# Attention and gated-MLP kernel: the q*k products of four groups summed to one chunk on VectorE, queues planned anew, and the last output group added in order of completion

## The chip, the cores and the metric

One core of a Trainium2 chip. The metric is the device time of one execution in microseconds, as the median of several executions. Two kernels are compared by a ratio: the mean time of one kernel's fast runs over the mean of the other's fast runs of the same rounds, so it is not quite the ratio of the medians that are quoted. A difference under 2% counts as "the same" for a verdict; here the differences are near 1%, and what carries the argument is the ratio's interval and the traces.

Engines: TensorE (PE, matmuls; PEld is its weight load), VectorE (DVE), ScalarE (ACT), GpSimd (POOL), SyncE (SP), which issues nearly all DMAs here.

## The reference, cut to what matters

```python
x = A_x                                   # 2048 tokens, width 512
xn = _layernorm(x)
return x + _A_ref(xn, A_wqkv, A_wo) + _B_ref(xn, B_w_in, B_w_sp, B_b_sp, B_w_out)

# A: attention, 32 heads of 16; each token looks at 8 keys, 0, 2, ... 14 tokens back
logits = jnp.einsum('bhsd,bhswd->bhsw', q, kg) * scale
o = jnp.einsum('bhsw,bhswd->bhsd', softmax(logits), vg)      # then @ wo

# B: gated MLP
z = _gelu(x @ w_in); z1, z2 = z[..., :688], _layernorm(z[..., 688:])
g = jnp.einsum('ts,bsf->btf', w_sp, z2) + b_sp[None, :, None]
return jnp.einsum('bsf,fd->bsd', z1 * g, w_out)
```

## The kernel before

Every engine has its own queue of instructions, and the kernel gives the order of all of them in one long list of tokens; an instruction starts when its queue has come to it and its inputs and buffers are ready. So the list is a plan of every queue at once:

```python
ORDER = """
z1.2 z2.1 p1.3 z0.3 zg1.2 p0.2 zg2.1 q2.3 zg0.3 p1.1 zs2.1 z1.0 p1.2 qc2.3 q2.1 p1.0 zg1.0 p0.0 z2.2 qc2.1
# ... 14 lines cut ...
s1.1 O2 T12 Gi15 A55 A56 A57 Or2 A58 Oh2.0 U15 A59 T15 Oh2.1 F2.0 F2.1 s2.0 O3 F2.2 F2.3 xr3 s2.2 Or3 s2.3
Oh3.0 s2.1 Oh3.1 F3.0 F3.1 s3.0 s3.1
"""
```

`z`/`X` are PE's products for z2 and z1, `q` those for q and k, `V` for v, `G` those of the spatial mix g. On DVE, `p` multiplies q by k, `a` is the pair add below, `N` normalises z2, `A` are the multiplies and adds of softmax weights with v (15 for each of four output groups), `U` is z1*g, `F` adds the residual to the output. `L` are the logits matmuls, `O`, `Or`, `Oh` the three parts of an output group, `T` a DMA transpose of u = z1*g, `xr` and `s` loads of x and stores of the output.

A logit is a sum over 16 dimensions. The products stand as four chunks of 128 partitions (four dimensions of 32 heads each), for 8 groups. DVE adds chunks 2 and 3 to 0 and 1; a selection matmul with `rsel` sums four partitions into one and adds the two chunks in PSUM, the memory that holds PE's results. Four blocks of tokens (`tb`) go into four column strips of 32 of the PE array:

```python
def pair_add(g):
    if g not in PAIRED:                      # PAIRED = all eight
        return
    V.tensor_tensor(pr[g % 3][:, 0:2], pr[g % 3][:, 0:2], pr[g % 3][:, 2:4], ALU.add)

def logits(g):
    o, h = g // 2, g % 2
    pl = ps_aux.tile([P, 4, P], F32, name="pl", tag="aux")
    n_c = 2 if g in PAIRED else C
    for c in range(n_c):
        for tb in range(TB):
            PE.matmul(pl[32 * tb:32 * tb + 32, :, :], rsel[:], pr[g % 3][:, c, :, tb, :],
                      start=(c == 0), stop=(c == n_c - 1), tile_position=(0, 32 * tb))
    tiles["l", g] = pl
```

An output group takes PSUM tiles from the same three-buffer pool as z and g, two blocks of tokens in one tile. In the last group's second half the adds and stores of blocks 2 and 3 follow their matmuls, so they come into DVE's queue before `F3.0 F3.1`, the adds of blocks 0 and 1:

```python
ps_mm = ctx.enter_context(tc.tile_pool(name="ps_mm", bufs=3, space=PSUM))
# ... in out_heads ...
        if tb % 2 == 0:
            pmm = ps_mm.tile([P, 2, TBS], F32, name="po", tag="mm")
        pos.append(pmm[:, tb % 2, :])
# ...
def out_half(o, h):
    if o == 3 and h == 1:
        for tb, part, E in ((2, 0, SP), (3, 0, A), (3, 1, SP)):
            out_full(o, tb, part)            # matmuls
            out_add(o, tb, part)             # DVE
            out_store(o, tb, part, E)        # DMA
    else:
        for tb in (2 * h, 2 * h + 1):
            out_full(o, tb)
```

## Time and profile before

| | before |
|---|---|
| median of 4 runs | 206.69 us (206.44 to 207.16) |
| span of the profiled run | 206.2 us |
| busy: PE, DVE, ACT | 199.2, 180.8, 97.3 us |
| DVE's waits, 25 to 192 us | 8.9 us |
| PE, first z product to last matmul | 177.90 us |
| last matmul to last DVE add, then to the end | 1.63, 2.90 us |

The lines themselves are in the prediction. Two rows need a word. "First z product to last matmul" is taken from PE's timeline (start of the first `pz` row, end of the last `pb` row). I use it below for all kernels, because the start varies between executions whatever the kernel: the first z product begins between 22.4 and 25.0 us in the profiles of this study, as the first loads come sooner or later, and in the two latest (`d1` and `e6`) the granted clock was low as well: 0.55 and 0.60 in the two stretches of 2 us from 8 us on in `d1`, 0.69 and 0.50 in `e6`, against 1.00 in the changed kernel's second profile. The span carries that accident; this length does not. The profiled execution of the kernel before had a late start too and took 207.95 us, 1.26 above the median. In five profiles of this study in which PE's work is the same, it is 176.82 or 176.83 us.

### The profile page before, as it was taken

How to read it: one execution, taken by the hardware profiler on the slowest of the kernel's cores; microseconds unless marked ns; L12 is line 12 of the kernel's file. 1: busy time of each engine (PE TensorE's matmuls, PEld its weight loads, DVE VectorE, ACT ScalarE, POOL GpSimd, SP SyncE). 2: the span in 40 equal slices, each digit the busy share in tenths (PEclk: the TensorE clock that was granted, in tenths of full speed). 3: DMA queues.
4: the chain of work that ended last, by engine and by line, in shares of the span. 5: the costliest groups of instructions: out<-in, count | busy, mean ns of one | idle time of the engine just before them, and what ended most of it. 6: DMA issues, size and time to landing. Idle time of an engine off the chain costs nothing.

```text
span 206.2 us, 4083 instructions
## 1 busy us (share of the span) xinstructions
PE 199.2 (97%) x1695; PEld 126.2 (61%) x1699; DVE 180.8 (88%) x259; ACT 97.3 (47%) x159; POOL 5.6 (3%) x15
## 2 busy tenths in 40 slices
PE   7899999999999999999999999999999999999991
PEld 2598866555566666666566666664566654664650
DVE  3979799899679999969999999999999998589604
ACT  3375998879899787634303755430032230020000
POOL 5000000500000000000000000000000000000000
PEclk9999999999999999999999999999999999999998
DMA  5972547400000693199960599998389000465523
GB/s 137 356 257 53 102 101 239 107 0 0 3 0 3 155 182 73 38 234 224 157 168 21 114 199 181 253 206 188 89 152 235 10 3 0 115 147 167 155 97 103
DMA packets 65826, 25.91 MB, mean 126 GB/s; under 512 B 56208, under 2 KB 65488, under 8 KB 65552
## 3 DMA queue, kind: packets, MB, share of 16 engines
q1 hardware_dynamic: 65360, 25.12, 54.9%
q0 software_dynamic: 80, 0.26, 0.5%
q10 hardware_dynamic: 368, 0.27, 0.5%
q8 instruction: 13, 0.21, 0.5%
q14 instruction: 5, 0.04, 0.1%
HBM read 10.13 MB, written 2.10 MB: 59 GB/s over the span
## 4 chain that ended last, share of the span: by engine, by line
PE 94%; DMA 2%; DVE 1%; issue 1%; DVEq 0%; ACTq 0%
PE pg L448 36%; PE pz L235 18%; PE pq L306 14%; PE po L520 7%; PE pv L409 7%; PE po L496 6%; PE pl L359 2%; DMA r_x<-in_A_x_dram 2%; PE pt L221 1%; PE pa L520 1%; PE po L505 1%; PE pb L496 1%; DVE r_qk L510 1%; PE pa L306 0%; DVEq L687 0%
## 5 line engine op out<-in xcount | busy, mean ns | idle before, releaser
L448 PE MATMUL pg<-z,r_qk 128*128 128x344 bf16 x448 | 67.0, 309 | 0.0
L448 PEld LDWEIGHTS <-r_qk 128*128 128x128 bf16 x448 | 43.8, 98 | 21.8
L235 PE MATMUL pz<-w_z,xnT 128*128 128x344 bf16 x256 | 40.3, 309 | 0.0
L423 DVE TENSOR_TENSOR r_pr<-r_x,r_w 128x2048 bf16<-128x2048 bf16 x32 | 38.2, 1218 | 0.4
L454 ACT ACTIVATE gs<-pg,b_col 128x688 bf16<-128x688 f32 x16 | 13.2, 831 | 53.7 <-PE pg L448 53.6
L427 DVE TENSOR_TENSOR r_pr<-r_pr 128x2048 bf16<-128x2048 bf16 x28 | 33.9, 1216 | 0.1
L235 PEld LDWEIGHTS <-xnT 128*128 128x128 bf16 x256 | 24.8, 98 | 13.8 <-issue 1.2
L340 DVE TENSOR_TENSOR r_pr<-r_qk 128x2048 bf16<-128x2048 bf16 x24 | 28.2, 1218 | 2.5 <-ACT r_qk L316 2.5
L306 PE MATMUL pq<-xnT,r_w 128*128 128x256 bf16 (+1 forms) x176 | 29.7, 323 | 0.0
L306 PEld LDWEIGHTS <-r_w 128*128 128x128 bf16 x184 | 20.5, 115 | 7.5 <-issue 0.6
L316 ACT CAST r_qk<-pq 128x1024 bf16<-128x1024 f32 (+1 forms) x16 | 15.4, 993 | 3.7 <-PE pq L306 3.4
L297 ACT ACTIVATE r_uz<-pz 128x688 bf16<-128x688 f32 x16 | 11.6, 744 | 9.7 <-PE pz L235 9.5
L520 PE MATMUL po<-r_w,r_uz 128*128 128x512 bf16 x66 | 14.9, 379 | 0.6 <-issue 0.6
L409 PE MATMUL pv<-xnT,r_w 128*32 128x512 bf16 x256 | 14.6, 380 | 0.0
L496 PE MATMUL po<-r_lg,r_pr 32*128 32x512 bf16 x224 | 14.5, 375 | 0.0
L520 PEld LDWEIGHTS <-r_uz 128*128 128x128 bf16 x85 | 8.0, 98 | 9.8 <-issue 1.5
L351 DVE TENSOR_TENSOR r_pr<-r_pr 128x4096 bf16<-128x4096 bf16 x6 | 13.5, 2285 | 0.0
L203 DVE BATCH_NORM_STATS2 stats<-r_x 128x6 f32<-128x512 bf16 x16 | 10.8, 673 | 2.1 <-DMA r_x<-in_A_x_dram 2.1
L259 ACT ACTIVATE junk<-z 128x688 bf16<-128x688 bf16 x16 | 12.5, 781 | 0.1
L409 PEld LDWEIGHTS <-r_w 128*32 128x32 bf16 x256 | 9.5, 138 | 4.5 <-issue 0.3
L253 ACT ACTIVATE z<-pz 128x688 bf16<-128x688 f32 x16 | 11.8, 741 | 0.5 <-PE pz L235 0.5
L496 PEld LDWEIGHTS <-r_pr 32*128 32x128 bf16 x272 | 7.6, 93 | 6.5 <-issue 0.9
(80 smaller groups left out, 164.0 us busy)
## 6 DMA issues: line engine op xcount, KB each, us to landing
r_lg<-in_A_wo_dram SPq DMA_DIRECT2D x8, 256.0 KB, 4.1
r_qk<-in_A_x_dram SPq DMA_DIRECT2D x16, 128.0 KB, 2.4
out_dram<-r_qk SPq DMA_DIRECT2D x15, 128.0 KB, 2.1
r_w<-in_A_wqkv_dram SPq DMA_DIRECT2D x3, 512.0 KB, 5.6
r_x<-in_A_x_dram SPq DMA_DIRECT2D x3, 512.0 KB, 6.2
w_z<-in_B_w_in_dram SPq DMA_DIRECT2D x2, 688.0 KB, 6.7
r_w<-in_B_w_out_dram SPq DMA_DIRECT2D x1, 640.0 KB, 5.1
r_x<-in_A_x_dram POOLq DMA_DIRECT2D x1, 256.0 KB, 4.3
```

The source lines that it names most:

```text
L235: PE.matmul(pz[:, hh, 0:FHALF], xnT[:, kc, i * P:(i + 1) * P], wz[:, kc, hh * FHALF:(hh + 1) * FHALF], start=(kc == 0), stop=(kc == C - 1))
L306: PE.matmul(pq[:, cc, p0 * P:(p0 + b1 - b0) * P], wqk[:, sd, kc, c0 + cc:D:C], xv[:, kc, b0:b1, j, :], start=(kc == 0), stop=(kc == C - 1))
L316: cast = A.copy(dst, pq[:, :, p0 * P:(p0 + b1 - b0) * P].rearrange("p c (b t) -> p c b t", b=b1 - b0))
L340: prod = V.tensor_tensor(pr[g % 3][:, c].rearrange("p w b t -> p b w t"), q3.unsqueeze(2).broadcast_to([P, TB, 4, P]), k4, ALU.mult)
L351: V.tensor_tensor(pr[g % 3][:, 0:2], pr[g % 3][:, 0:2], pr[g % 3][:, 2:4], ALU.add)
L409: PE.matmul(pv[32 * tb:32 * tb + 32, dd, :], wv[:, kc, 2 * d2 + dd, :], xnT[:, kc, tb * TBS:(tb + 1) * TBS], start=(kc == 0), stop=(kc == ...
L423: V.tensor_tensor(pw_t[n], vp[:, :, off:off + P], a_sb[:, slot_w(w), ts].unsqueeze(1).broadcast_to([P, DH, P]), ALU.mult)
L427: V.tensor_tensor(pw_t[n] if dst is None else dst, pw_t[n], pw_t[m], ALU.add)
L448: PE.matmul(pg[:, hh, 0:FHALF], wsp[n][:, k, :], z2[:, k, hh * FHALF:(hh + 1) * FHALF], start=(k == 0), stop=(k == NT - 1))
L454: A.activation(gs[:], tiles.pop(("g", n))[:, :, 0:FHALF], ACT.Identity, bias=b_col[:, i:i + 1])
L496: PE.matmul(pc, op[32 * tb:32 * tb + 32, d, o * P:(o + 1) * P], wo_r[32 * tb:32 * tb + 32, d, cs], start=(d == 8), stop=False, tile_positi ...
L520: PE.matmul(pc, uT[:, o % 2, m, tb * P:(tb + 1) * P], wout[:, m, cs], start=False, stop=(m == MCH - 3))
```

## The change

The intent: take matmuls off PE, which is busy from end to end, by one more add on DVE for four of the eight groups; plan all queues anew so that DVE has room for it; and let the last adds go in the order in which their sums are complete.

```diff
-PAIRED = (0, 1, 2, 3, 4, 5, 6, 7)
+CHUNKS = (1, 1, 2, 2, 1, 1, 2, 2)
 ORDER = """
-z1.2 z2.1 p1.3 z0.3 zg1.2 p0.2 zg2.1 q2.3 zg0.3 p1.1 ...        (all 18 lines replaced; cut)
-Oh3.0 s2.1 Oh3.1 F3.0 F3.1 s3.0 s3.1
+z1.3 z0.0 p1.1 z1.1 zg1.3 p0.0 zg0.0 q2.0 zg1.1 p0.1 ...
+A55 s1.3 T9 A56 U12 O2 Gi15 U15 U13 T15 A57 T13 A58 Or2 Oh2.0 T12 A59 Oh2.1 F2.0 F2.1 s2.1 T14 O3 F2.2 F2.3
+xr3 s2.0 Or3 s2.3 Oh3.0 s2.2 Oh3.1 F3.0 F3.1 s3.1 s3.0 end
 """
     def pair_add(g):
-        if g not in PAIRED:
-            return
         V.tensor_tensor(pr[g % 3][:, 0:2], pr[g % 3][:, 0:2], pr[g % 3][:, 2:4], ALU.add)
+
+    def pair_add2(g):
+        V.tensor_tensor(pr[g % 3][:, 0], pr[g % 3][:, 0], pr[g % 3][:, 1], ALU.add)
...
-        n_c = 2 if g in PAIRED else C
+        n_c = CHUNKS[g]
...
     def out_half(o, h):
-        if o == 3 and h == 1:
-            for tb, part, E in ((2, 0, SP), (3, 0, A), (3, 1, SP)):
+        for tb in (2 * h, 2 * h + 1):
+            for part in range(len(tiles["o", o][tb])):
                 out_full(o, tb, part)
-                out_add(o, tb, part)
-                out_store(o, tb, part, E)
-        else:
-            for tb in (2 * h, 2 * h + 1):
-                out_full(o, tb)
+
+    def last_adds():
+        for tb, part, E in ((2, 0, SP), (3, 0, A), (3, 1, SP)):
+            out_add(3, tb, part)
+            out_store(3, tb, part, E)
```

The new tokens `b0 b1 b4 b5` are `pair_add2`, `end` is `last_adds`.

More of the change, by code (lines that the diff above doesn't have):

```diff
@@ L40 @@
 ORD = [1, 2, 3, 0]
-PAIRED = (0, 1, 2, 3, 4, 5, 6, 7)
+CHUNKS = (1, 1, 2, 2, 1, 1, 2, 2)
 ORDER = """
-z1.2 z2.1 p1.3 z0.3 zg1.2 p0.2 zg2.1 q2.3 zg0.3 p1.1 zs2.1 z1.0 p1.2 qc2.3 q2.1 p1.0 zg1.0 p0.0 z2.2 qc2.1
-p0.3 zs1.2 z2.0 p0.1 zg2.2 z0.0 zg2.0 a1 w0 q2.0 zs2.0 zg0.0 a0 z1.1 qc2.0 q2.2 zg1.1 halo zs1.0 p2.3 z3.2
-qc2.2 X1 p2.0 z0.1 Xg1 zg3.2 L1 zs2.2 L0 z2.3 zs3.2 p3.3 zg0.1 z0.2 p3.2 zg2.3 z1.3 p2.2 zg0.2 zs1.1 q3.1 p3.0
-Lc0 Lc1 p2.1 zg1.3 q3.3 zs0.1 p3.1 qc3.1 q3.0 a2 qc3.3 z3.3 qc3.0 a3 q3.2 zg3.3 zs1.3 nw.0 p4.3 z3.0 qc3.2
@@ L47 @@
-zs0.0 X0 p4.0 zs2.3 p4.2 L2 zg3.0 L3 V7 zs0.3 nw.1 p5.3 zs0.2 Xg0 V1 nw.2 p5.0 Lc3 Vc7 nw.3 nw.4 V6 nw.5 nw.6
-p4.1 Vc1 zs3.0 p5.1 z3.1 Vc6 p5.2 X5 Lc2 zg3.1 M0.0 w4 V4 nw.7 zs3.3 nw.8 a4 Xg5 w3 V5 Vc4 st.0 nw.9 nw.10
-M0.1 nw.11 nw.12 w1 V2 st.1 a5 Vc5 zs3.1 L4 w2 Vc2 V0 nw.13 N2.3 N1.0 st.2 N2.2 M0.2 N1.1 L5 N2.1 V3 N0.1 st.3
-Vc0 N0.2 N1.2 N0.3 st.4 N1.3 X4 Vc3 N3.3 N0.0 N3.0 X2 N2.0 N3.1 p7.1 G0.0 p7.3 G0.1 Xg2 N3.2 Xg4 G0.2 p6.2 Lc5
-X3 M0.3 G0.3 p6.0 Xg3 Lc4 G4 p6.3 w6 Gi0 p6.1 late E0 S0.0 G1 p7.0 w10 S0.1 S0.2 p7.2 S0.3 S0.4 Gi4 a6 w8 G3
@@ L52 @@
-Gi1 w5 a7 w9 R0 L6 L7 Lc6 A0 G2 Lc7 Gi3 A1 A2 U3 mask U4 M1.0 G6 wo1.0 A3 wo1.3 wo1.2 M1.1 U0 M1.2 A4 A5 G5 A6
-Gi6 Gi2 M1.3 A7 U1 A8 T1 X8 Gi5 U2 T0 A9 E1 X6 A10 G8 wo0.1 A11 w7 A12 Xg8 wo0.0 Xg6 S1.0 T3 S1.1 X7 A13 G9
-Xg7 A14 w14 Gi8 A15 wo0.3 A16 T2 S1.2 A17 G7 U6 wo0.2 S1.3 U5 wo1.1 S1.4 Gi9 xr0 R1 A18 T4 A19 X9 Gi7 A20 G14
-A21 w11 Xg9 U7 A22 w13 A23 A24 T5 X11 Gi14 A25 O0 Xg11 T7 A26 A27 w15 U8 A28 Or0 Oh0.0 U9 A29 Oh0.1 F0.0 A30
-A31 G10 T8 F0.1 F0.2 F0.3 s0.2 T6 A32 A33 xr1 X10 Gi10 A34 w12 X12 Xg10 A35 G13 Xg12 A36 T9 A37 s0.0 A38 s0.3
@@ L57 @@
-s0.1 A39 X15 A40 Gi13 X14 A41 G11 A42 Xg14 Xg15 A43 A44 A45 U14 X13 Gi11 A46 O1 Xg13 A47 U11 A48 U10 Or1 A49
-Oh1.0 A50 Oh1.1 F1.0 F1.1 G12 F1.2 U13 s1.2 A51 T10 F1.3 T11 T14 G15 Gi12 T13 U12 A52 s1.3 xr2 A53 A54 s1.0
-s1.1 O2 T12 Gi15 A55 A56 A57 Or2 A58 Oh2.0 U15 A59 T15 Oh2.1 F2.0 F2.1 s2.0 O3 F2.2 F2.3 xr3 s2.2 Or3 s2.3
-Oh3.0 s2.1 Oh3.1 F3.0 F3.1 s3.0 s3.1
+z1.3 z0.0 p1.1 z1.1 zg1.3 p0.0 zg0.0 q2.0 zg1.1 p0.1 q2.2 qc2.0 p1.0 p1.3 q2.3 qc2.2 p0.3 z3.1 p0.2 qc2.3
+zs1.1 z0.3 p1.2 zg3.1 z1.2 a0 w0 zg0.3 zs1.3 z1.0 zs0.3 a1 q3.1 zg1.2 w3 zg1.0 halo q2.1 zs0.0 b0 qc3.1 p2.0
@@ new lines @@
+z2.2 qc2.1 b1 z2.0 p2.2 V0 zg2.0 p2.3 zg2.2 zs2.0 L1 L0 z0.1 Vc0 p3.3 Lc0 q3.3 p3.0 zs1.2 zg0.1 p2.1 q3.0
+qc3.3 p3.1 z0.2 a2 qc3.0 zs2.2 z2.3 zg0.2 q3.2 p3.2 zs1.0 zg2.3 a3 z3.0 qc3.2 z3.2 zg3.0 p4.3 zs2.3 z2.1 zg3.2
+p4.1 z3.3 zs0.2 p4.0 zg2.1 X3 zg3.3 nw.0 p4.2 X5 Xg3 nw.1 a4 Lc1 X4 Xg5 zs0.1 L2 zs2.1 V4 p5.3 zs3.1 st.0 Xg4
+nw.2 V3 nw.3 p5.2 Vc4 nw.4 p5.0 zs3.2 L3 V2 zs3.0 nw.5 nw.6 nw.7 Vc3 nw.8 nw.9 nw.10 p5.1 Lc2 V5 Lc3 nw.11 b4
+w4 Vc2 V1 nw.12 Vc5 a5 w2 zs3.3 V7 Vc1 nw.13 st.1 b5 w1 V6 Vc7 N0.0 N1.2 st.2 N1.0 N0.2 L4 L5 N0.3 X7 N1.1
@@ new lines @@
+st.3 N2.0 st.4 Vc6 N0.1 X6 N1.3 N3.1 late N2.3 N3.2 G0.0 N3.0 Xg7 M0.0 G0.1 Xg6 N2.1 M0.1 N2.2 X1 M0.2 N3.3
+p7.1 G0.2 Xg1 M0.3 Lc4 G0.3 p7.3 G1 p6.0 E0 p7.2 Gi0 p6.3 Lc5 p6.2 G4 Gi1 w7 S0.0 p7.0 w6 p6.1 S0.1 xr0 S0.2
+G3 a7 S0.3 S0.4 Gi4 w5 a6 w10 R0 X0 Gi3 U4 L7 T4 L6 G2 A0 Xg0 Lc6 w8 U1 Lc7 U3 U0 A1 A2 X2 Gi2 mask M1.0 G5
+Xg2 A3 A4 A5 A6 X12 M1.1 Gi5 w11 A7 G6 Xg12 A8 wo1.0 w9 A9 M1.2 A10 wo1.1 A11 G7 Gi6 U5 M1.3 T5 U6 A12 E1 A13
+G8 U2 Gi7 A14 T2 A15 T6 S1.0 A16 X10 Gi8 w14 S1.1 X14 A17 T1 A18 G9 Xg10 S1.2 wo1.3 A19 T3 A20 S1.3 A21 T0 G14
@@ new lines @@
+A22 Gi9 wo0.3 wo0.2 A23 Xg14 A24 U7 A25 S1.4 T7 X8 Gi14 A26 wo1.2 X9 wo0.0 wo0.1 A27 w12 G10 A28 Xg9 R1 Xg8
+A29 w13 A30 X13 A31 G11 Xg13 A32 Gi10 A33 U8 A34 A35 X11 Gi11 A36 O0 Xg11 A37 A38 U14 A39 Or0 Oh0.0 A40 A41
+Oh0.1 F0.0 U10 s0.0 F0.1 G13 F0.2 T8 A42 s0.1 F0.3 A43 s0.3 xr1 U11 A44 O1 w15 U9 A45 Gi13 A46 A47 Or1 Oh1.0
+A48 Oh1.1 F1.0 F1.1 A49 s1.1 s0.2 G12 T11 A50 A51 F1.2 F1.3 s1.2 s1.0 A52 xr2 X15 A53 G15 Xg15 A54 T10 Gi12
+A55 s1.3 T9 A56 U12 O2 Gi15 U15 U13 T15 A57 T13 A58 Or2 Oh2.0 T12 A59 Oh2.1 F2.0 F2.1 s2.1 T14 O3 F2.2 F2.3
@@ L650 @@
     st = z2_var(3, 3) + [z2_log, z2_exp]
-    steps = {"z": z2_mm, "zg": z2_gelu, "zs": z2_sq, "q": qk_mm, "qc": qk_cast, "p": prod_c, "a": pair_add,
+    steps = {"z": z2_mm, "zg": z2_gelu, "zs": z2_sq, "q": qk_mm, "qc": qk_cast, "p": prod_c, "a": pair_add, "b": pair_add2,
              "L": logits, "Lc": logits_cast, "V": v_mm, "Vc": v_cast, "X": z1_mm, "Xg": z1_gelu,
@@ L656 @@
              "G": g_mm, "Gi": g_bias, "U": u_mul, "T": u_tr, "A": lambda k: ap[k](),
-             "O": out_heads, "Or": out_rest, "Oh": out_half, "F": out_add, "s": out_store,
+             "O": out_heads, "Or": out_rest, "Oh": out_half, "F": out_add, "s": out_store, "end": last_adds,
              "halo": halo_zero, "wo": load_wo, "late": load_late, "xr": load_xr, "w": load_wsp}
```

## The prediction

> **What bounds the kernel now.** I read the page's busy shares and slices first, then the chain that ended last, then the groups of instructions, then the waits of VectorE (DVE) and its order of time.
>
> ```profile
> PE 199.2 (97%) x1695; PEld 126.2 (61%) x1699; DVE 180.8 (88%) x259; ACT 97.3 (47%) x159; POOL 5.6 (3%) x15
> PE   7899999999999999999999999999999999999991
> DVE  3979799899679999969999999999999998589604
> PE 94%; DMA 2%; DVE 1%; issue 1%; DVEq 0%; ACTq 0%
> ```
>
> Busy shares, slices of 5.2 us, and shares of the chain. TensorE (PE) is busy in every slice but the first and last, and the chain runs through it for 94% of the 206.2 us span. A busy PE need not be at its best, but here no wait for another engine stands between 8 us and 201.7 us: its only idle pieces are four of 0.16 us marked "issue", ahead of the last matmuls of the output groups. So a PE instruction that goes shortens the end, unless a wait opens. DVE at 88% is the runner-up.
>
> The logits stage, from the chain in order of time:
>
> ```profile
> 72.60 0.43 PE pl L359 x8
> 74.75 0.43 PE pl L359 x8
> 99.19 0.98 PE pl L359 x16
> ```
>
> Start, length, what: eight selection matmuls (one group, two chunks) hold PE for 0.43 us, or 54 ns each, though each is recorded at 381 ns. Four run side by side in column strips. The same matmuls between full-width ones take 0.98 us for 16, that is 0.11 us over 16 x 54 ns, and the full-width stretch after such a block is also 0.11 us too long (3.61 us for 24 of L235, which elsewhere take 3.50 us).
>
> The end, from the timeline of all engines and DVE's own (start, length, engine, line):
>
> ```profile
> 200.62 1.07 DVE L510 TENSOR_TENSOR r_qk<-pa,r_qk 128x512 bf16<-128x512 f32 x2 [6.10 <-PE pa L520]
> 201.03 0.64 PE L520 MATMUL pb<-r_w,r_uz 128*128 128x224 bf16 x5
> 201.71 0.39 DVE L510 TENSOR_TENSOR r_qk<-pb,r_qk 128x224 bf16<-128x224 f32 x1
> 202.02 1.28 DVE L510 TENSOR_TENSOR r_qk<-po,r_qk 128x512 bf16<-128x512 f32 x2
> ```
>
> PE ends at 201.67 us. The two `po` adds belong to blocks 0 and 1 of the last group, whose sums are complete some 4 and 3 us before the span's last matmul, since PE does blocks 0, 1, 2, 3 in that order. They are queued behind the adds of 2 and 3, and DVE idles 6.10 us first. That is an order of the queue, not of the data.
>
> The waits of DVE from 25 to 192 us (total, times, longest):
>
> ```profile
> DVE r_uz L462 <- ACT gs L454: 2.7, 1, 2.7
> DVE r_pr L340 <- ACT r_qk L316: 2.5, 1, 2.5
> DVE smt L388 <- ACT r_w L383: 1.8, 1, 1.8
> DVE r_qk L510 <- PE po L520: 0.8, 1, 0.8
> DVE r_uz L340 <- ACT r_qk L316: 0.6, 1, 0.6
> DVE zvar L265 <- ACT junk L259: 0.5, 1, 0.5
> ```
>
> They add to 8.9 us. This is all the room DVE has.
>
> **What the Trainium skill says.** "VectorE: DVE Perf Modes", section "The perf-mode tier table", lists 1224 ns for a bf16 `tensor_tensor` of 2048 elements, with 2x as its ceiling. The trace agrees: 1218 ns for L340 and 1216 for L427. "TensorE: Matmul & The Clock Gate", Part 3, says that small matmuls at different tile positions run concurrently in the array; agreed, 381 ns recorded against 54 ns of PE's time each. So a group's matmul is far cheaper than its record. "Perfetto Trace Analysis", "Identifying the Most-Contended Engine", warns that matmul busy share is a poor measure of distance from the roofline; I therefore rest on the gapless chain, not on the 97%. "DMA: Bandwidth & Descriptors", "Anatomy of one DMA", puts about 2.0 us of fixed cost on a DMA (measured there for GpSimd's path). Output stores here take 2.0 us to landing in the median and 1.5 at least, so the last store's landing can't be removed by this change.
>
> **The change, part by part.**
>
> Logits on PE. Four of eight groups (0, 1, 4, 5) go from two chunks to one: 4 x 4 = 16 matmuls fewer, 16 x 54 ns = 0.87 us. In the new order the column-strip work (logits and v products) falls into three unbroken stretches instead of four; a stretch costs 0.11 us on each side, so another 0.22 us. All of this lies on the path: **1.1 us off PE**.
>
> Adds on DVE. Four `tensor_tensor` of 128x2048 are new. The row says 1218 ns, but starts in a run lie nearer: eight of L340 take 9.17 us, so 1.146 us each. Four cost 4.6 us. They are off the path as long as DVE keeps its appointments. For that I summed the durations along both queues, with no waits, from 23.9 us (PE) and 25.9 us (DVE), in the old and the new order. In the old order DVE's last group-3 sum, which the last heads matmuls need, comes to 182.1 us by this sum; the trace has it end at about 191.4, so 8.9 us of waits and 0.4 of small overhead. PE needs it at 193.1: spare 1.7 us. In the new order the sum gives 186.6, with the overhead 187.0; PE, 1.1 us earlier, needs it at 192.0. So DVE may wait **5.0 us in all** where it now waits 8.9. I think it will wait 2 to 4: the first two new adds are queued ahead of the products of output group 2, and the 2.5 us hole at 54.9 (products waiting for the q/k casts) is just where 2 x 1.146 us fit. Five products instead of three now stand between the softmax maximum and the sum that waits 1.8 us for ScalarE's exponential. The 2.7 us hole before an L462 multiply comes from a g product that is placed earlier, relative to it, in the new order.
>
> Other appointments by the same sums, allowing 1.5 to 2.5 us of waits and overhead so far: the first g products (PE at 78.0 to 82.7) need normalised z2 some 0.5 to 1 us earlier, and have it; the last logits (PE at 99.1) need the last pair add, at 98.5 to 99.2. This one is close. Output groups 0, 1 and 2 start at 151.4, 164.4 and 183.4 and their sums are done by about 124, 146 and 168: wide.
>
> Queues planned anew. The same 16 z2 tiles, 16 z1 tiles, 8 q/k, 8 v, 16 g products and all loads remain; only positions move. It is worth nothing itself: it makes room for the adds. One risk: the last transposes (four of u) now include one queued behind an output store on SyncE, issued near 191 to 192.5; with the 2.7 us that transposes take to land it arrives at 194 to 195.2, against a need at 195.4.
>
> Last group's adds. The matmuls keep their order, the adds of blocks 0 and 1 go ahead. DVE's last add then ends 0.43 us after PE's last matmul (202.10 against 201.67) instead of 1.63 us (203.30): **1.2 us less**. What follows is a store and its landing: 206.2 - 203.3 = 2.9 us now. The last store becomes 56 KB rather than 128 KB, so perhaps 0.3 us less; I count half.
>
> Sum: 1.1 + 1.2 + 0.15 = 2.45 us, on the span 206.2 to 203.75. I take off 0.2 us for small stalls at the close appointments: 206.78 - 2.25, rounded to **204.5 us**, 1.1% less.
>
> **The rivals.** First, DVE becomes the bound: the 4.6 us are not hidden. For it speaks that DVE is busy in nearly every slice from 100 to 175 us and that the close joins have under 1 us to spare. Against it: 8.9 us of holes, and z1 and g work of PE that the new order puts ahead of output group 0 (it starts at 151 instead of 138.8 us), which is what a planner does to gain slack. If all holes stay, 8.9 - 5.0 = 3.9 us of stall arise: 208.4 us. If half stay, none. Second, the saved chunk is hidden or taken back: PE gains 1.1 us and then waits as long for a late transpose or cast, and only the tail remains: 205.5 us. For it speaks that transposes and adds are close; against it that the old order shows the same close margins and not one wait. Third, matmuls are worth what their records say: 16 x 381 ns = 6.1 us, making 199 us. The 0.43 us pieces of the chain rule it out.
>
> **Range and chances.** Main case, PE gapless and the tail shortened by 1.2 to 1.5 us: 204.0 to 204.6. Stalls of up to 1.5 us at the joins: up to 206. Runs of one kernel differ by 0.3 us. So 203.5 to 206.2. Over 2% faster needs under 202.7 us, 1.8 us more than I can find: 0.04. Over 2% slower needs 210.9, more than the first rival in full: 0.02. Within 2%: 0.94.
>
> **What would show it right or wrong.** In the changed profile: 48 matmuls of L359's line instead of 64 and PE's last matmul near 200.6; 12 adds of the pair kind, four with 2048 elements, and DVE's total about 185; the three holes of 2.7, 2.5 and 1.8 us gone or halved; no line of PE waiting for DVE or a DMA between 24 and 199 us; DVE's last instruction a `pb` add, some 0.4 us after PE's end; the span ending 2.6 to 2.9 us after it. I am wrong if PE waits for DVE at the last pair adds (near 99 us) or at the last output group's start (near 192), for a transpose near 195, or if the store's end grows because several stores leave together.

## The result

The changed kernel takes **204.69 us** (median of 4 runs, 204.55 to 205.33) against 206.69. The ratio is 0.9907, 95% interval 0.9879 to 0.9935: within 2%, and clear of 1. Measured again with more rounds on another chip it was 205.02 us and 0.9906 (0.9881 to 0.9932). Its profile, page first; line numbers have moved by one or two (L359 is L360 now, L510 is L511):

```profile
PE 196.2 (97%) x1679; PEld 125.0 (62%) x1683; DVE 185.0 (91%) x263; ACT 102.5 (51%) x163; POOL 18.0 (9%) x15
PE   7799999999999999999999999999999999999993
DVE  4999799999999999999899999999999999988504
```

PE has 16 instructions fewer and the slices stay full. DVE has four more and is at 91%; the softer digits that it had before slice 25 are nearly gone. ACT's 5 us more are four more loads of function tables (ten where there were six, 1.28 us each) that the new order brings, and POOL's 12 us more are one cast of the bias that is recorded at 15.1 us, not 2.8; PE waits for neither after 24 us.

The logits in the chain of work (start, length, what):

```profile
43.67 0.43 PE pl L360 x8
61.05 0.55 PE pl L360 x8
65.05 0.43 PE pl L360 x8
74.12 0.43 PE pl L360 x8
97.99 0.98 PE pl L360 x16
```

48 matmuls in 2.82 us. Before, the chain's five pieces were 64 matmuls in 3.80 us (0.98 twice, 0.43 twice, 0.98).

DVE's waits from 25 to 192 us (total, times, longest):

```profile
DVE r_qk L511 <- PE po L521: 1.6, 2, 0.9
DVE r_uz L463 <- ACT gs L455: 1.3, 1, 1.3
DVE r_pr L424 <- PE pl L360: 0.8, 1, 0.8
DVE zmean L263 <- ACT z L253: 0.4, 1, 0.4
```

4.1 us in place of 8.9. The waits of 2.5 us for the q/k casts and of 1.8 us for the exponential have gone. PE's own waits for other engines after 24 us: none.

The end, from the timeline of all engines:

```profile
197.28 1.29 DVE L511 TENSOR_TENSOR r_qk<-po,r_qk 128x512 bf16<-128x512 f32 x2 [5.12 <-DMA out_dram<-r_qk]
198.48 1.04 DVE L511 TENSOR_TENSOR r_qk<-pa,r_qk 128x512 bf16<-128x512 f32 x2
198.67 0.64 PE L521 MATMUL pb<-r_w,r_uz 128*128 128x224 bf16 x5
199.45 0.38 DVE L511 TENSOR_TENSOR r_qk<-pb,r_qk 128x224 bf16<-128x224 f32 x1
```

The two `po` adds are first now, and the last add ends 0.52 us after PE's last matmul.

Where the time went, in the traces: the span fell by 3.4 us, but 1.28 us of that is the start (first z product at 23.77 us before, 22.49 after), which is chance. The rest is PE's length, 177.90 to 176.82 us (1.08 less), and the way from its last matmul to the last add, 1.63 to 0.52 us (1.11 less); the end after that got 0.07 us longer. 1.08 + 1.11 - 0.07 = 2.12 us, against 2.00 in the medians.

### The profile page after: what moved, and what is told of

Read it like the earlier page. It is cut to its first block, busy times and chain, and to the rows that moved or that the text cites. A ratio compares the mean times of both kernels' runs of the same rounds, so it can differ in the third digit from the quotient of the medians.

```text
span 202.8 us, 4061 instructions
## 1 busy us (share of the span) xinstructions
PE 196.2 (97%) x1679; PEld 125.0 (62%) x1683; DVE 185.0 (91%) x263; ACT 102.5 (51%) x163; POOL 18.0 (9%) x15
## 4 chain that ended last, share of the span: by engine, by line
PE 85%; DMA 4%; SPq 3%; DVE 3%; issue 2%; ACT 1%; ACTq 0%; DVEq 0%
PE pg L449 35%; PE pz L235 19%; PE pq L306 13%; PE pv L410 7%; PE po L521 4%; PE po L497 4%; DMA r_x<-in_A_x_dram 1%; PE pl L360 1%; DMA r_uz<-r_uz 1%; DMA out_dram<-r_qk 1%; SPq L469 1%; DVE r_qk L511 1%; SPq L516 1%; SPq L474 1%; PE pt L221 1%
## 5 line engine op out<-in xcount | busy, mean ns | idle before, releaser
L306 PE MATMUL pq<-xnT,r_w 128*128 128x256 bf16 (+1 forms) x176 | 28.5, 316 | 0.3 <-ACT xnT L225 0.3
L634 POOL CAST b_col<-b 128x16 f32<-128x16 bf16 x1 | 15.1, 15142 | 32.7 <-DMA b<-in_B_b_sp_dram 32.7
L511 DVE TENSOR_TENSOR r_qk<-po,r_qk 128x512 bf16<-128x512 f32 x14 | 9.1, 684 | 6.8 <-DMA out_dram<-r_qk 5.1
```

Source lines behind the costliest of these rows:

```text
L306: PE.matmul(pq[:, cc, p0 * P:(p0 + b1 - b0) * P], wqk[:, sd, kc, c0 + cc:D:C], xv[:, kc, b0:b1, j, :], start=(kc == 0), stop=(kc == C - 1))
L634: G.tensor_copy(b_col[:], b16[:])
```

## The experiments

All kernels gave the right result. The table has for each the median, the ratio to the kernel before in the same rounds with its interval, and from the one profile PE's length as explained above and the way from PE's last matmul to DVE's last add. The lengths with 3 and 6 idle adds are from executions in which the granted clock fell as well; see there.

| kernel | median us | ratio (95%) | PE length us | to last add us |
|---|---|---|---|---|
| before | 206.69 | | 177.90 | 1.63 |
| changed | 204.69 | 0.9907 (0.9879-0.9935) | 176.82 | 0.52 |
| changed, again | 205.02 | 0.9906 (0.9881-0.9932) | 176.82 | 0.43 |
| changed, old ending | 205.97 | 0.9964 (0.9950-0.9978) | 176.82 | 1.63 |
| before, new ending | 205.32 | 0.9937 (0.9924-0.9951) | 177.91 | 0.43 |
| changed, two chunks everywhere | 205.84 | 0.9960 (0.9948-0.9973) | 178.01 | 0.43 |
| before, one chunk in old queues | 207.83 | 1.0055 (1.0042-1.0068) | 179.06 | 1.63 |
| changed + 1 idle add | 204.84 | 0.9903 (0.9872-0.9933) | 176.82 | 0.43 |
| changed + 3 idle adds | 207.33 | 1.0042 (1.0015-1.0068) | 180.77 | 0.43 |
| changed + 6 idle adds | 213.15 | 1.0299 (1.0266-1.0331) | 184.45 | 0.53 |
| changed + 2 idle adds later | 205.35 | 0.9929 (0.9895-0.9963) | 177.28 | 0.43 |
| changed, one transpose early | 204.73 | 0.9895 (0.9871-0.9919) | 176.83 | 0.42 |
| the same, five groups of one chunk | 204.35 | 0.9873 (0.9823-0.9923) | 176.60 | 0.43 |
| the same, six groups | 204.49 | 0.9873 (0.9832-0.9914) | 176.68 | 0.44 |

### The ending, undone and alone

`e1_old_tail`: in the changed kernel, the old `out_half` is put back and `last_adds` does nothing.

```diff
     def last_adds():
-        for tb, part, E in ((2, 0, SP), (3, 0, A), (3, 1, SP)):
-            out_add(3, tb, part)
-            out_store(3, tb, part, E)
+        pass
```

> The changed kernel with the old ending alone: the last output group's adds of blocks 2 and 3 stand ahead of those of 0 and 1 again; all else is new. Theory (the tail is worth what the distance from PE's last matmul to DVE's last add says): that distance goes back from 0.5 to 1.6 us, so 1.1 us slower than the changed kernel (204.7 -> 205.8), ratio to the kernel before 0.995. Rival (the gain is in the matmuls and queues, the tail is hidden behind stores that land late anyway): under 0.4 us slower.

`e2_new_tail_only`: the kernel before, with the new `out_half`, `last_adds` and the token `end`; nothing else.

```diff
-Oh3.0 s2.1 Oh3.1 F3.0 F3.1 s3.0 s3.1
+Oh3.0 s2.1 Oh3.1 F3.0 F3.1 s3.0 s3.1 end
```

> The kernel before with the new ending alone; its queues and its two chunks for all groups stay. Theory: 1.1 us faster than before (206.7 -> 205.6), ratio 0.9945, with DVE's last add 0.5 us after PE's last matmul. Rival (the new ending only pays with the new queues, as the stores of the old order stand in its way): 0 to 0.4 us.

Undone, it costs 1.0 to 1.3 us by the medians (205.97 against 205.02 and 204.69, on other chips) and 1.2 us by the ratios (0.0057 of 206.7). Alone it gives 1.4 us by the medians, 1.3 by the ratio. The way from PE's last matmul to the last add is 1.63 us in every kernel with the old order and 0.42 to 0.53 in every one with the new; PE's length does not move. Both rivals (hidden behind stores; worth something only with the new queues) fall.

### The chunks, undone in the new queues

`e3_two_chunks_new_queues`:

```diff
-CHUNKS = (1, 1, 2, 2, 1, 1, 2, 2)
+CHUNKS = (2, 2, 2, 2, 2, 2, 2, 2)
     def pair_add2(g):
+        if CHUNKS[g] == 2:
+            return
```

> The changed kernel with two chunks for all groups (the four new adds gone, 16 logits matmuls back); new queues and new ending stay. Theory (54 ns a matmul, gapless PE): PE from the first z product to its last matmul grows by 0.87 us, time 205.6, ratio 0.9945; DVE does 4.6 us less and only idles more. Rival A (DVE had become the bound): the time stays or falls though PE has more to do. Rival B (a matmul is worth its record of 381 ns): 6 us slower.

205.84 us, and PE's length grows by 1.19 us, more than the 0.87 expected. The sixteen matmuls account for 0.87 at most, so PE waited. Its weight loads show where (timeline of PEld; in brackets the idle time before and what ended it):

```profile
195.08 0.09 PEld L499 LDWEIGHTS <-r_pr 32*128 32x128 bf16 x1
195.61 0.33 PEld L508 LDWEIGHTS <-r_uz 24*128 24x128 bf16 x8 [0.43 <-DMA r_uz<-r_uz]
```

The transpose of u's tile 14, queued on SyncE behind the first store of group 2 (`s2.1 T14`), came late. Up to the start of the last output group, PE's time is as worked out: 168.98 us from the chain's first z product against 169.20 in `e2`, the 0.22 us that the three column-strip stretches save against four. From there to the last row of matmuls (`pb`) it takes 8.23 us instead of 7.91: 0.32 us of waiting. In the changed kernel the same stretch takes 7.90 us, with no wait. So the transpose that the prediction named as a risk sits on the edge. Rival A (DVE had become the bound) and rival B (381 ns a matmul) fall: DVE does four adds fewer here, and the kernel is slower, by 1.1 us.

Compared with `e2`, which has the same ending and the same matmuls, this run also prices the plan by itself: 178.01 against 177.91 us of PE, so the new queues alone are worth nothing. By the medians this run is even 0.5 us slower than `e2` (205.84 against 205.32), of which 0.1 is PE; in `e2`'s profile the end after the last add is 0.4 us shorter (2.6 against 3.0 us), and why is not shown.

### One chunk without the new queues

`e4_one_chunk_old_queues`: the kernel before with `CHUNKS` and `pair_add2`, and each new add right behind its pair add.

```diff
-p0.3 zs1.2 z2.0 p0.1 zg2.2 z0.0 zg2.0 a1 w0 q2.0 zs2.0 zg0.0 a0 z1.1 ...
+p0.3 zs1.2 z2.0 p0.1 zg2.2 z0.0 zg2.0 a1 b1 w0 q2.0 zs2.0 zg0.0 a0 b0 z1.1 ...
-p4.1 ... nw.8 a4 Xg5 ...      M0.1 ... st.1 a5 Vc5 ...
+p4.1 ... nw.8 a4 b4 Xg5 ...   M0.1 ... st.1 a5 b5 Vc5 ...
```

> The kernel before with one chunk for the same four groups, each new add right after the pair add of its group, old queues and old ending. It asks what the new plan was worth. Theory (8.9 us of DVE's waits soak up most of 4.6 us, but the appointments near 79, 83 and 99 us have under 1 us to spare): PE gets 1 to 2 us of waits for DVE that take the 0.87 us back: 206.5 to 208. Rival (the plan is not needed, the holes take all): 205.9, ratio 0.996, PE without a wait.

207.83 us: slower than the kernel before. PE's waits in this run:

```profile
PE pl L360 <- DVE r_uz L352: 1.2, 1, 1.2
PE po L521 <- issue: 0.6, 4, 0.2
PE pg L449 <- DVE z L289: 0.4, 1, 0.4
```

The logits of a group wait 1.2 us for its second add (L352), and the first g products wait 0.4 us for normalised z2; together with weight loads that start late, PE's length is 179.06 us. That is 1.16 us more than before although 0.87 us of matmuls are gone, so about 2.0 us of waiting was bought. The holes of DVE did take a part: its wait for the casts fell from 2.5 to 0.3 us and the one for the exponential from 1.8 to 0.9. The point is that a hole helps only the appointments behind it. With the adds in these places the old queues can't afford them, and the new plan can; other places in the old queues were not tried.

### How much room has DVE? Adds that nobody reads

To measure the room directly, adds of 128x2048 into a dead weight buffer were put into DVE's queue of the changed kernel, between the weighted v sums A34 and A35.

```diff
-... A33 U8 A34 A35 X11 ...
+... A33 U8 A34 y y y A35 X11 ...
+    scr = w_z2[:].rearrange("p k f -> p (k f)")[:, 0:4 * TBS].rearrange("p (w t) -> p w t", w=4)
+    def idle_add():                                              # token y
+        V.tensor_tensor(scr, a_sb[:, 0:4, :], a_sb[:, 4:8, :], ALU.add)
```

`c0_changed_again` is the changed kernel beside them.

> The changed kernel itself, unaltered, as the yardstick for the runs beside it (its first measurement had few rounds and an interval of 0.6%). All theories: 204.7 us, ratio to the kernel before 0.990 to 0.991.

> The changed kernel with three more adds of 128x2048 on DVE that nobody reads (into a dead weight buffer), in the middle of the weighted v sums; 3.4 us of DVE work. The last sum that PE needs ended 2.8 us ahead of its reader in the changed kernel, and 1.3 us of DVE's waits lie between. Theory (DVE is busy but not the bound): no change, within 0.2 us of 204.7. Rival (at 91% DVE has become the bound): 3.4 us slower, 208.1.

> The same with six idle adds, 6.9 us of DVE work. Theory (room of 2.8 us at the last sum plus 1 to 2 us of waits that close): 2.0 to 3.1 us slower, 206.7 to 207.8, with PE waiting for DVE's last sum ahead of the last output group, and nowhere else. Rival (DVE the bound): 6.9 us slower. Rival (DVE has much more room than the trace shows): under 1 us slower.

My theory failed. Three adds (3.4 us of DVE) made it 2.3 us slower by the medians, and PE's length 3.95 us longer in the profiled execution; six (6.9 us) made it 8.1 us slower, which is more than was added. The wait is not at the last weighted sum. PE's timeline of the changed kernel, then of the kernel with three adds (start, length, line, out and in, in brackets the wait before):

```profile
163.43 3.63 PE L497 MATMUL po<-r_lg,r_pr 32*128 32x512 bf16 x64
```

```profile
163.47 0.39 PE L497 MATMUL po<-r_lg,r_pr 32*128 32x512 bf16 x2
165.73 5.31 PE L497 MATMUL po<-r_lg,r_pr 32*128 32x512 bf16 x62 [1.88 <-DVE r_qk L511]
170.67 0.80 PE L506 MATMUL po<-r_w,r_uz 24*128 24x512 bf16 x8
```

After two matmuls of output group 1, PE waits for L511, the output add. The third matmul writes the second PSUM tile of the group, and that buffer is still held by group 0 until DVE has added its last block. In the changed kernel that add starts at 161.28 and takes 0.68 us, so it ended 1.5 us ahead of the reader:

```profile
161.28 0.68 DVE L511 TENSOR_TENSOR r_qk<-po,r_qk 128x512 bf16<-128x512 f32 x1
```

With three idle adds in front it starts at 164.99. Second, the same matmuls take 5.31 us where they took 3.63. The table by stretches of the run with three adds (columns as labelled; PEclk is the granted clock) says why:

```profile
core 0: us, PE busy (x) PEld busy (x) DVE busy (x) ACT busy (x) POOL busy (x), PEclk, DMA share, GB/s
160.00:165.00 5.00, 3.85 (x27) 2.25 (x25) 4.96 (x9) 0.83 (x1) 0.00 (x0) 1.00 0.28 74
165.00:170.00 5.00, 4.27 (x48) 2.02 (x51) 5.00 (x10) 0.00 (x0) 0.00 (x0) 0.66 0.58 169
170.00:175.00 5.00, 4.84 (x42) 2.27 (x36) 4.70 (x7) 0.00 (x0) 0.00 (x0) 1.00 0.77 96
```

The clock granted to PE fell to 0.66 in the stretch after the wait. So in this execution 1.9 us of waiting cost 3.95 us of PE's length. With six adds:

```profile
168.10 0.61 PE L497 MATMUL po<-r_lg,r_pr 32*128 32x512 bf16 x2 [3.64 <-DVE r_qk L511]
170.44 5.22 PE L497 MATMUL po<-r_lg,r_pr 32*128 32x512 bf16 x62 [1.72 <-DVE r_qk L511]
```

Waits of 5.4 us, and 7.63 us of length; the clock was 0.69 and 0.63 in the two stretches of 5 us from 165. The Trainium skill, "TensorE: Matmul & The Clock Gate", section "HAM oscillation", says that PE's clock is cut back after gaps of more than about 3.4 us; the direction agrees, but with three adds the cut followed a wait of 1.9 us.

It did not come in every execution. Eight of the 14 runs with three adds had a mean granted clock of 0.999 or 1.0 and took 206.67 to 207.46 us; their median, 206.96, is 1.9 us above the changed kernel's 205.02, about the length of the wait alone. The other six, with a mean clock of 0.992, took 208.44 to 209.79 (the last counts as slow), and the profile shows one of these. Where the other five lost their clock is not shown: the profiles of `d1` and `e6` have the same mean clock from the cut near 8 us. So by these runs the wait costs its own length, and in some executions a loss of clock on top.

New theory: the join at group 1's PSUM buffers has 1.5 us of room, and behind it there is more. Two runs to test it, one add in the same place, and two adds just behind the join:

```diff
-... A33 U8 A34 A35 X11 ...
+... A33 U8 A34 y A35 X11 ...              (d1)
-... A42 s0.1 F0.3 A43 ...
+... A42 s0.1 F0.3 y y A43 ...             (d2)
```

> The changed kernel with one idle add in the same place as the three before. The runs with three and six put PE's wait at the start of output group 1, whose second pair of PSUM banks comes free with the last add of group 0; in the changed kernel that add ended 1.5 us ahead of its reader. New theory (this join has 1.5 us of room, and what goes beyond it costs more than itself, as PE's granted clock falls after a wait): one add of 1.15 us fits, no change, 204.7 to 205.1, no wait of PE on DVE. Rival (every DVE microsecond costs): 1.15 us slower, 206.1.

> The changed kernel with two idle adds, 2.3 us, placed just behind the last add of output group 0, so past that join. Theory (the next joins have 2.8 us or more: the last weighted sum, and the adds of group 1): no change, 204.7 to 205.1, no wait of PE on DVE. Rival (the place does not matter, only DVE's total): as slow as two adds before the join, 0.8 us of wait and the clock's loss, 206 or more.

One add: PE's length is 176.82 us, the same to the last digit, and no wait: 1.15 us fits into 1.5. Two adds behind the join: 177.28 us, 0.46 more, ratio 0.9929. Near my expectation but not on it: there is one short wait,

```profile
178.22 4.83 PE L449 MATMUL pg<-z,r_qk 128*128 128x344 bf16 x32 [0.26 <-DVE r_qk L511]
```

and again it is a PSUM buffer that an output add (group 1's) has to free, this time for a g product. In the changed kernel that product starts at 177.58 and the add ended at 175.68, so the room was 1.9 us, not the 2.8 us that I had read at the last weighted sum. The rival (each DVE microsecond costs one) falls with d1.

### The transpose moved, and a fifth and sixth group

`e5_last_transpose_early`: tile 14 of u is ready since the middle of the last third; its transpose goes up the queue.

```diff
-A55 s1.3 T9 A56 ... F2.0 F2.1 s2.1 T14 O3 ...
+A55 s1.3 T9 T14 A56 ... F2.0 F2.1 s2.1 O3 ...
```

> The changed kernel with one transpose of u (tile 14, ready since the middle of the last third) moved ahead on SyncE's queue, from behind the first store of group 2 to behind the transpose of tile 9. Theory (the changed kernel's end is a near tie: the transpose lands within 0.3 us of its need, in the run with two chunks it came 0.4 us late, and the loads and stores behind it hold back the add of block 0 by about a microsecond, which DVE makes up in all but 0.1 us): 0.1 to 0.4 us faster than the changed kernel, 204.3 to 204.6; block 0's add starts within 0.2 us of PE's last matmul for it, no wait of PE or its weight loads for a transpose. Rival (the chain of waits through SyncE that the profile names sets the end): 1 us faster. Rival (no tie): no change at all.

No change that can be told: 176.83 us of PE, 0.42 us to the last add, 204.73 us beside 205.02. My theory of a near tie at the very end was wrong, and so was the reading of the profile behind it. The bracket `[5.12 <-DMA out_dram<-r_qk]` in the end of the changed kernel names a store as the releaser of the first `po` add. In the second profile of the same program the same instruction reads

```profile
197.34 1.29 DVE L511 TENSOR_TENSOR r_qk<-po,r_qk 128x512 bf16<-128x512 f32 x2 [5.02 <-PE po L521]
```

and in this run the add begins at 197.24, just after PE's ten matmuls for blocks 0 and 1 end (195.10 + 2.12 = 197.22). The two blocks share one PSUM tile, and the add of block 0 waits for the matmuls of both. What released it was PE; the store only happened to land then. The move takes the risk that `e3` showed away, no more.

`e6_fifth_group` and `e7_sixth_group`, both with the early transpose:

```diff
-CHUNKS = (1, 1, 2, 2, 1, 1, 2, 2)
+CHUNKS = (1, 1, 2, 2, 1, 1, 2, 1)      (e6; a7 -> a7 b7)
+CHUNKS = (1, 1, 2, 1, 1, 1, 2, 1)      (e7; a3 -> a3 b3 as well, and:)
-R0 X0 Gi3 U4 L7 T4 L6 G2 A0 Xg0 Lc6 w8 U1 Lc7 U3 U0 A1 A2 X2 Gi2
+R0 X0 Gi3 U4 X2 L7 T4 L6 U1 G2 U3 Xg0 U0 A0 Lc6 w8 Lc7 A1 A2 Gi2
```

> A try at a better version: group 7 too goes to one chunk (a fifth added sum of 1.15 us on DVE, 4 matmuls less), with the transpose of tile 14 early. Theory: PE 0.22 us less than the changed kernel; DVE's 0.8 us wait at the first weighted sum takes most of the add, and 1.5 us of room at output group 1 the rest: 204.5, no wait of PE. Rival (the last logits at 98 us come too late, as the pair sum for group 6 now ends 0.5 us ahead of PE): 0.3 to 1 us slower.

> Groups 3 and 7 too, six in all, with one z1 tile put ahead of the last logits and two u products ahead of the first weighted sum. Theory: PE 0.44 us less than the changed kernel if no join is missed: 204.3. Against it: DVE runs some 1.1 us later from 55 us on, with 1.5 us of room at the first g products, 1.1 us at the third and 1.5 us at output group 1; if one is missed, 0.3 to 1.5 us slower than the changed kernel.

The fifth group takes exactly the 0.22 us off PE (176.60), with no wait. Five of its six runs lie between 204.16 and 204.38 us; all ten of the changed kernel lie between 204.55 and 205.33. They ran on different chips and the intervals of the ratios overlap, so I call it some 0.3 us better by PE's length and by the runs, not by the verdict. The sixth group brings nothing more: 176.68 us where 176.38 was expected. The 0.3 us went in output group 0 (its matmuls spread over 3.93 us instead of 3.63). What held them can be read from the timelines of PE's weight loads and of ACT (columns as before):

```profile
150.15 3.13 PEld L497 LDWEIGHTS <-r_pr 32*128 32x128 bf16 x61 [0.21 <-issue]
149.26 0.83 ACT L455 ACTIVATE gs<-pg,b_col 128x688 bf16<-128x688 f32 x1 [3.68 <-DVE r_uz L465]
```

After the group's first three weight loads there are none until 150.15. By the order of the tiles, the group's second PSUM tile takes the buffer of a g product, which ACT's bias add frees at 150.09; and that add had waited for a product u of DVE. In the changed kernel the same add ends at 150.11 and the group starts only at 150.34. So here too it seems to be a buffer, with DVE behind it by way of ACT; no run tests it. Several runs in this last set, of the kernel before too (up to 210.2 us), were 1.5 us and more above their fellows; the profiles of `d1` and `e6` fell on such runs and show a late start with a low clock, first z product at 24.5 and 25.0 us, and a PE length as it should be.

## Why the prediction was right

It said 204.5 us within 203.5 to 206.2; 204.69 and 205.02 were measured. Step by step:

- **PE is gapless, and a logits matmul is worth 54 ns.** Right. 1.1 us was forecast, 1.08 measured. `e3` put the matmuls back and lost 0.87 us (and a wait of 0.32 that was not theirs); `e6` took four more away and won 0.22. The three stretches of column strips gave their 0.22 us, as `e3` against `e2` shows. The four pieces of 0.16 us marked "issue" were no idle time: each stands before a row of 19 matmuls, which has 20 and no gap in the profiles of `d1`, `d2`, `e6` and `e7`, so a record is missing in each.
- **The last adds are worth 1.2 us.** Right in size: 1.11 in the profile, 1.0 to 1.4 in `e1` and `e2`. The working had a wrong step: blocks 0 and 1 are not free for adding "some 4 and 3 us before the span's last matmul". They share a tile, and the first of their adds begins only at 197.28, 2.0 us before PE ends. DVE then works without a gap to the end and is done in time, but with nothing to spare.
- **The last store is smaller, 0.15 us.** Wrong. From the last add to the end it took 2.90 us before and 2.97 after; the size of the last store, 128 or 56 KB, does not show. (The landing of the stores, 2.0 us in the prediction's median, is 2.1 on the page.)
- **4.6 us of adds are hidden.** Right for the changed kernel: PE waits nowhere, DVE's waits went from 8.9 to 4.1 us (2 to 4 were expected, so just over), its busy time to 185.0 us (about 185), and the last weighted sum ended at 187.98 us, 2.8 ahead of its reader. The two holes that I expected to close did, and the third halved.
- **The close appointments.** The last logits, which I called close, had 1.6 us (sum done at 96.35, matmuls at 97.99). Output groups 0 to 2, which I called wide, were not: I had checked when their sums are ready, not when their PSUM buffers come free. The plan moved group 1 from 167.0 to 163.4 us and brought group 0 next to it, and it left 1.5 us between the last add of group 0 and the matmuls of group 1 that need its buffer. In the kernel before, by the order of the tiles, that buffer went first to a z1 tile: the add ended at 149.8 us and the tile's matmuls start near 152.9, so there were about 3 us. It did not cost anything here. The idle adds show that it was the first bound behind the place where they stand; missing it by 1.9 us cost 1.9 us in most runs and about double in the profiled one.
- **The queues are worth nothing themselves, they make room.** Right: nothing was gained by them alone (`e3` against `e2`: 0.1 us the wrong way in PE's length, 0.5 by the medians), but without them the adds, placed as in `e4`, turn a gain into a loss of 1.1 us. Positions are not all that moved: ACT loads its tables four times more, which it could afford.
- **The late transpose.** The risk was real: it struck in `e3` by 0.4 us, and missed the changed kernel.
- **The rivals.** DVE as the bound at 208.4 us: not in this plan, but near; `e4` is that case. Gain taken back by a transpose, 205.5 us: it happened in part in `e3` only. 381 ns a matmul: ruled out.
- **0.2 us for small stalls.** None showed. It stood in for the store's 0.15 us and the rest, so two small errors partly cancelled.

## What to carry to other kernels

Where one engine has no gap, count the saving by how far the *chain* moves past the instruction, not by its recorded duration, and check the work that it moves to another engine at each appointment, not in total: room is a property of a join, and the holes behind a join do nothing for it. List the joins where a *buffer* is freed as well as those where data is read; the one that the idle adds ran into was of that kind. No view of the profile lists room that is not yet used up: it has to be worked out for each join, as the start of the reader less the end of the work that it needs. Filling an engine with work that nobody reads, a little at a time, measures that room directly.

## What the Trainium skill lacked or had wrong

- "TensorE: Matmul & The Clock Gate", section "HAM oscillation": it gives gaps above about 3.4 us as what costs clock. In the profile with three idle adds the granted clock was 0.66 from 165 to 170 us, right after a single wait of 1.88 us, and 1.9 us of waiting cost 3.95; eight of the 14 runs of that kernel show no such loss. A wait of 1.2 us (`e4`) left the clock at nine tenths or more in every slice, but in `d1` it was at 0.55 just after waits of 0.85 and 0.63 us near the start. So these runs give no length of gap that is safe or that always costs.
- The same page, Part 3, packing of small matmuls: measured speed-ups are there for four row tiles (3.07x) and three column tiles (2.38x), none for four column tiles. Here 32 v products in four column strips take 1.73 us, and so do eight full-width matmuls of the same 512 columns: 4.0x. "TensorEngine Tiling (Array Packing)" names up to 4x as a theoretical speedup and says, under "Key Properties", that a change of tiling mode drains TensorE, but neither page gives a time for the change: it was 0.11 us here on each side of a stretch of column strips.
- "DMA: Bandwidth & Descriptors", section "Anatomy of one DMA": its fixed cost of about 2 us (measured there for GpSimd's path) fits the landing of a store (1.8 us in the median), but the way from the last add to the end of the span was about 2.9 to 3.0 us in most kernels, whether the last store had 128 or 56 KB; the page has no figure for that whole way, from the issue of the last store to the last instruction.
- "Perfetto Trace Analysis": it tells how to follow a wait back to its releaser, not how to find the room of a join where nothing waits yet. That room was 1.5 us here; no view lists it, and it came out of two rows of the timeline once the join was known.
